# Channel mixing's first layer by fifteen products for 3x3x2 blocks, and forms of both layers' weights in one series

## The chip, the cores and the metric

The kernel runs on one core of a Trainium2 chip, as one launch. The metric is the device time of one execution in microseconds (us), the median of several runs. TensorE (PE) does the matmuls, VectorE (DVE), ScalarE (ACT) and GpSimd (POOL) the elementwise work, and SyncE (SP) issues most transfers.

## The reference

Attention with normalized queries and keys for 8 batch elements and 12 heads (448 positions, 64 wide), then a mixer over its result, all in float32:

```python
q_n, k_n = (rmsnorm(q, g_q), rmsnorm(k, g_k))        # over the 64
scores = scale * np.matmul(q_n, k_n.transpose(0, 1, 3, 2))
attn = softmax(scores); attn_out = np.matmul(attn, v)
x = attn_out.transpose(0, 2, 1, 3).reshape(8, 448, 768)
xt = x.transpose(0, 2, 1)
h = np.maximum(xt @ w_tok1, 0.0) @ w_tok2            # token mixing, 448 -> 256 -> 448
u = x + h.transpose(0, 2, 1)
h2 = np.maximum(u @ w_ch1, 0.0) @ w_ch2              # channel mixing, 768 -> 1536 -> 768
return u + h2
```

The mixer's weights arrive as float64.

## The kernel before

The elements go through one after another. For each: attention in six blocks of two heads (scores L458, exponentials on ACT L462, row sums of them added on DVE in `es` L499, the product with v L531; then the sums' transpose `dt` L560, reciprocal `rc` L562, its transpose `rd` L574 and the scaled result `uT` L577); `x` in the other orientation through DRAM (`send_x` L786, `load_x` L795); token mixing `tok1` (L837, L844) and `tok2` (L879, drained at L884); channel mixing `ch1` (L999) and `ch2` (L1065). The attention of the next element is laid between the products of channel mixing, in blocks: `place` puts the six blocks ahead of the products whose numbers `BLOCKS` lists, counted over both layers. Each of PE, DVE, ACT and POOL works in the order in which the program is written. `later(t, fn)` puts off work to a time of a modelled PE clock, and the order in SP's queue is set by a planner from such times.

Element 0's channel mixing is plain (`first_stage`, L969, 36 products): meanwhile float64 weights are loaded (`weight_load` L222, into five `raw` tiles) and converted on DVE and ACT (L345 to L379). Converted weights go to DRAM scratch (`store`), and come back as units of 384 KB (`unit`, L927, eight buffers).

From element 1 on `ch1` is made in 3 times 7 products of 12 matmuls of 224 columns, the products of a 2x2x2 block scheme. For these, sums of weights are made once on POOL (`sum_items`; the first eight, `few`, in tiles of the pool of `x` during element 0, with loads on POOL's own queue), and sums of the moving data each element (`moving_sums` L900 to L904, tile `tu`). Results pile up by `PRODUCTS` in `hb` and `r`; drains on DVE (L1005), copies on ACT (L1009, L1021), relu on ACT (L1006).

`ch2` is plain in element 1 (`plain_2`, L1048), and from element 2 on 15 products of 8 matmuls of 224 columns, for 3x3x2 blocks: `ch2(b, f, x)` for f in 0 to 14 and x in 0, 1, drained by `C_STEPS[f]` (L1076, L1080). Its moving operands, forms of the hidden layer, are made in place by `x_form` (L1039, 896 elements) as `X_STEPS` lists them; the first four of them are written after products 0, 2, 3 and 5 of the last block of `ch1`. The forms of its weights (8 groups of 16 operations and 4 copies, L320, L324, sent at L310) are made on POOL in `form_items`, during element 1.

Two pools of PSUM tiles matter here: `m_tile` (two tiles; all products of `ch1` and `ch2`) and `s_tile` (four; scores and transposes). `put_off` holds back work until the next product's matmuls are written.

Of the kernel before, what the change touches and what calls it, by code (L numbers as in the profile page):

```python
# [8 lines left out]
F32 = mybir.dt.float32  # L9
# [13 lines left out]
NQ = 8  # L23
NF9 = 15
# [16 lines left out]
    ("ch1", 0): (("v", 6, 1, "+", 3),), ("ch1", 2): (("v", 7, 6, "+", 0),),  # L41
    ("ch1", 3): (("g", 9, 0, "+", 1),), ("ch1", 5): (("v", 8, 7, "+", 2),),
# [20 lines left out]
    (("v", (1, 0), (1, 0), "+", "P"),))  # L63

# [19 lines left out]
def whole(ctx, tc, shifted, pre, q, k, v, g_q, g_k, moe_w_tok1, moe_w_tok2, moe_w_ch1, moe_w_ch2, out):  # L84
# [10 lines left out]
    P = 128  # L95
# [52 lines left out]
    ws1 = dram.tile([KF // 2, NQ, P, KC, 2, P], F32, name="ws1")  # L148
# [76 lines left out]
    def slots(j, lo, hi):  # L225

        w, group, m, t = stages[j]
        return ws1[group, lo:hi, :, t, m % 2, :].rearrange("q p n -> p q n")

    def store(j):  # L230

        w, group, m, t = stages[j]
        if group < 3:
            nc.sync.dma_start(out=slots(j, 0, 4), in_=st["stage", j])
            return
        to = wp2[:].rearrange("p (m q t) n -> p q m t n", m=KC, q=4)[:, :, m, t, :]
        nc.sync.dma_start(out=to, in_=st["stage", j])

    def has(group, made):
        return all(j in made for j, s in enumerate(stages) if s[1] == group)  # L240

    def sum_items():


        n = len(stages)

        def make(e, a, q):

            e.tensor_tensor(out=q[:, 6], in0=a[:, 1], in1=a[:, 0], op=ALU.subtract)
            e.tensor_tensor(out=q[:, 4], in0=a[:, 1], in1=a[:, 3], op=ALU.add)  # L250
            e.tensor_tensor(out=q[:, 5], in0=q[:, 6], in1=a[:, 3], op=ALU.add)
            e.tensor_tensor(out=q[:, 7], in0=a[:, 2], in1=q[:, 5], op=ALU.subtract)

        def send(i, e=nc.sync):
            st["summed"].add(i)
            e.dma_start(out=slots(i, 4, 8), in_=eight(st.pop(("sum", i)))[:, 4:8])


        FEW = 8

        def some(i):
            if 2 <= i:
                send(i - 2, nc.gpsimd)
            if i < FEW:
                t = st["sum", i] = x_pool.tile([P, KC, NS, P], F32, name="few", tag="x")
                nc.gpsimd.dma_start(out=eight(t)[:, 0:4], in_=slots(i, 0, 4))
            if 1 <= i <= FEW:
                q = eight(st["sum", i - 1])
                make(nc.gpsimd, q, q)

        order = list(range(FEW, n // 2))

        def one(i):
            if i < len(order):
                t = st["sum", order[i]] = raw_tile()
                nc.sync.dma_start(out=eight(t)[:, 0:4], in_=slots(order[i], 0, 4))
            if 0 <= i - 2 < len(order):
                q = eight(st["sum", order[i - 2]])
                make(nc.gpsimd, q, q)
            if 0 <= i - 3 < len(order):  # L280
                send(order[i - 3])
                load_units(st["at"])

        def eight(t):
            if len(t.shape) == 4:
                return t[:].rearrange("p j c n -> p (j c n)")[:, 0:NQ * P].rearrange("p (q n) -> p q n", q=NQ)
            return t[:].rearrange("p n w -> p (n w)").bitcast(F32).rearrange("p (q n) -> p q n", q=NQ)
        return ([(0.0, lambda i=i: some(i)) for i in range(FEW + 2)],
                [(1.0, lambda i=i: one(i)) for i in range(len(order) + 3)])

    def form_items():


        G, FORMS_FROM, FORMS_EVERY = range(8), 55.0, 18.0
        plain = lambda g: wp2[:].rearrange("p (m h x k t) n -> p x h t m k n", m=3, h=2, x=2, k=3)[
            :, g // 4, g // 2 % 2, g % 2]
        made = ws2[:].rearrange("p (f c) n -> p c f n", c=8)
        eight = lambda t: t[:].rearrange("p n w -> p (n w)").bitcast(F32).rearrange("p (q n) -> p q n", q=8)

        def load(g):  # L300
            a, b, c = st["form", g] = [eight(raw_tile()) for _ in range(3)]
            src = plain(g)
            for m in range(2):
                nc.sync.dma_start(out=a[:, 3 * m:3 * m + 3], in_=src[:, m])
            nc.sync.dma_start(out=a[:, 6:8], in_=src[:, 2, 0:2])
            nc.sync.dma_start(out=b[:, 7], in_=src[:, 2, 2])

        def send(g):
            a, b, c = st.pop(("form", g))
            nc.gpsimd.dma_start(out=made[:, g, 0:8], in_=c)  # L310
            nc.gpsimd.dma_start(out=made[:, g, 8:NF9], in_=b[:, 0:7])
            st["formed"] += 1

        def part(g, i):
            a, b, c = st["form", g]
            at = dict(d=a[:, 4], s=a[:, 6], v=a[:, 7], y=a[:, 3])
            at.update({(m, k): a[:, 3 * m + k] if 3 * m + k < 8 else b[:, 7] for m in range(3) for k in range(3)})
            at.update({f: c[:, f] if f < 8 else b[:, f - 8] for f in range(NF9)})
            for o, x, op, y in W_STEPS[4 * i:4 * i + 4]:
                nc.gpsimd.tensor_tensor(  # L320
                    out=at[o], in0=at[x], in1=at[y], op=ALU.add if op == "+" else ALU.subtract)
            if i == 3:
                for f, x in W_SINGLE:
                    nc.gpsimd.tensor_copy(out=at[f], in_=at[x])  # L324
                send(g)

        for g in G:
            at = FORMS_FROM + g * FORMS_EVERY
            later(at, lambda g=g: load(g))
            for i in range(4):  # L330
                later(at + 8.0 + 2.5 * i, lambda g=g, i=i: part(g, i))
# [472 lines left out]
    def trans_x(b, j):  # L804
# [20 lines left out]
        if o == KC - 1:  # L825
            t = st["xt"][:, half].rearrange("p j s -> p (j s)")
            if half:
                st.pop("xt")
            start, step, load = {(1, 1): (2.0, 0.5, 9.0), (2, 1): (2.0, 0.5, 9.0)}.get((b, half), (2.0, 2.0, 12.0))
            later(start, lambda: send_x(b, half, t, step))  # L830
            later(load, lambda: load_x(b, half))
# [58 lines left out]
    PRODUCTS = ((0, "B11"), (2, "B21"), (5, "T2"), (6, "T3"), (4, "T1"), (7, "B22"), (3, "T4"))  # L890

    def moving_sums(b, t):

        if t == 0:
            st["tu"] = tu_pool.tile([P, 4, KC, HS], F32, name="tu", tag="tu")
        u, tu = st["uT", b], st["tu"]
        B11, B12 = u[:, t, 0:HS], u[:, t, HS:S]
        B21, B22 = u[:, KC + t, 0:HS], u[:, KC + t, HS:S]
        T1, T2, T3, T4 = (tu[:, i, t, :] for i in range(4))
        nc.vector.tensor_tensor(out=T1, in0=B12, in1=B11, op=ALU.subtract)  # L900
        nc.vector.tensor_tensor(out=T2, in0=B22, in1=T1, op=ALU.subtract)
        e = nc.vector if b == 1 else nc.gpsimd
        e.tensor_tensor(out=T3, in0=B12, in1=B22, op=ALU.subtract)
        e.tensor_tensor(out=T4, in0=B21, in1=T2, op=ALU.subtract)  # L904

    def unit_list(b):

        flat = lambda a: a.rearrange("p a b n -> p (a b n)")
        l = [(mp, q < 4, flat(ws1[mp, q])) for mp in range(KF // 2) for q, _ in PRODUCTS]
        six = lambda w, i: w[:, 6 * i:6 * i + 6, :].rearrange("p a n -> p (a n)")  # L910
        if b == 1:
            return l + [(3, True, six(wp2, mt % KC * 4 + 2 * h + mt // KC)) for mt in order_2 for h in range(2)]
        return l + [(4, False, six(ws2, i)) for i in range(NF9 * 8 // 6)]

    def load_units(u):
# [3 lines left out]
        while ("stage", len(stages) - 1) in st["used"] and st["loaded"] < min(u + UNITS - 1, len(units)):  # L919
            i = st["loaded"]  # L920
            group, plain, src = units[i]

            if not plain and not (has(group, st["summed"]) if group < 3 else st["formed"] == 8):
                assert i > u
                break
# [61 lines left out]
    def ch1(b, mp, i):  # L987

        put_off_done()
        u, tu = st["uT", b], st["tu"]  # L990
        ps = m_tile()
        w = next_unit()
        q, what = PRODUCTS[i]
        for j in range(2):
            for t in range(KC):
                m = {"B11": u[:, t, 0:HS], "B21": u[:, KC + t, 0:HS], "B22": u[:, KC + t, HS:S]}.get(what)
                if m is None:
                    m = tu[:, int(what[1]) - 1, t, :]
                nc.tensor.matmul(  # L999
                    out=ps[:, j * HS:(j + 1) * HS], lhsT=w[:, t, j, :], rhs=m,  # L1000
                    start=(t == 0), stop=(t == KC - 1))
        got = ps[:, 0:2 * HS]
        h = {name: hb[:, 2 * mp + n, 2 * o:2 * o + 2, :].rearrange("p m n -> p (m n)")
             for name, o, n in (("B11", 0, 0), ("B12", 0, 1), ("B21", 1, 0), ("B22", 1, 1))}
        add = lambda e, o, x, y: e.tensor_tensor(out=o, in0=x, in1=y, op=ALU.add)  # L1005
# [520 lines left out]
```

## Time and profile before

| | us |
|---|---|
| median of 3 runs | 1286.82 (1285.78 to 1289.69) |
| profiled execution, its own time | 1290.15 |
| its span, first to last instruction | 1288.2 |
| PE busy | 1251.4 |
| DVE busy | 794.4 |
| ACT busy | 392.2 |
| POOL busy | 381.7 |

The mean granted clock of TensorE was 0.994. Element 0 ends at about 262 us, element 1 at about 424, and each of elements 2 to 6 takes about 148. The profile is of one execution; "busy" is the time in which an engine has an instruction in work, and a group's line gives its count, its busy time and the mean of one in ns, and then the engine's idle time ahead of it with what ended that.

### The profile page before, as it was taken

What the parts mean: (1) busy time and instruction counts of PE and PEld (TensorE: products, weight loads), DVE (VectorE), ACT (ScalarE), POOL (GpSimd) and SP (SyncE); (2) the same over time, 40 slices, a digit from 0 to 9 for tenths busy, and PEclk for the clock granted to TensorE, in tenths of its full rate; (3) what the DMA queues carried; (4) which work ended last, traced back from release to release, by engine and by line L of the source; (5) the groups of instructions that cost most, each with busy time, mean ns of one, the idle gap of its engine ahead of it and who ended that gap; (6) DMA issues with size and microseconds to landing.
All of it is one profiled execution on the core that took longest, in us unless ns stands there. A gap on an engine that the chain in (4) does not pass through costs nothing.

```text
span 1288.2 us, 20010 instructions
## 1 busy us (share of the span) xinstructions
PE 1251.4 (97%) x7228; PEld 890.5 (69%) x7228; DVE 794.4 (62%) x1229; ACT 392.2 (30%) x781; POOL 381.7 (30%) x641
## 2 busy tenths in 40 slices
PE   5998999999999999999999999999999999999996
PEld 3444444457744488796778777885787868797996
DVE  6987877846764355855668356765658366544243
ACT  5663333223331144402442043312343033200210
POOL 1303350024996611331223112241122222131231
PEclk9998999999999999999999999999999999999999
DMA  9666494999899876695658767685766864386553
GB/s 209 170 183 184 124 258 115 208 253 250 225 249 239 182 170 165 141 253 116 160 148 184 183 147 179 146 231 115 178 163 149 223 146 135 117 210 156 173 173 82
DMA packets 492864, 228.37 MB, mean 177 GB/s; under 512 B 375508, under 2 KB 453332, under 8 KB 492756
## 3 DMA queue, kind: packets, MB, share of 16 engines
q1 hardware_dynamic: 476178, 213.10, 67.2%
q0 software_dynamic: 3584, 12.06, 3.1%
q10 hardware_dynamic: 12994, 1.84, 0.8%
q8 instruction: 59, 0.97, 0.3%
q14 instruction: 49, 0.40, 0.1%
HBM read 184.26 MB, written 42.66 MB: 176 GB/s over the span
## 4 chain that ended last, share of the span: by engine, by line
PE 84%; DVE 7%; DMA 3%; SPq 2%; issue 1%; ACT 1%; POOL 0%; DVEq 0%; ACTq 0%; POOLq 0%
PE m_ps L999 25%; PE m_ps L1065 21%; PE s_ps L458 9%; PE o_ps L531 9%; PE m_ps L879 5%; PE m_ps L969 5%; PE t_ps L837 2%; PE m_ps L837 2%; PE m_ps L1048 1%; PE m_ps L511 1%; PE d_ps L511 1%; DMA x<-xs 1%; PE t_ps L432 1%; DVE es L499 1%; DVE raw L348 1%
## 5 line engine op out<-in xcount | busy, mean ns | idle before, releaser
L1065 PE MATMUL m_ps<-hb,unit 128*128 128x224 f32 x1440 | 277.2, 354 | 0.0
L1065 PEld LDWEIGHTS m_ps<-hb,unit 128*128 128x128 f32 x1440 | 270.9, 190 | 8.8 <-issue 7.7
L999 PE MATMUL m_ps<-tu,unit 128*128 128x224 f32 x1008 | 201.6, 355 | 1.3 <-ACT r L1009 1.3
L999 PEld LDWEIGHTS m_ps<-tu,unit 128*128 128x128 f32 x1008 | 189.1, 190 | 15.0 <-issue 9.2
L462 ACT ACTIVATE e<-s_ps 128x448 f32<-128x448 f32 x294 | 138.2, 550 | 179.1 <-PE s_ps L458 170.7
L999 PE MATMUL m_ps<-uT,unit 128*128 128x224 f32 x756 | 151.2, 354 | 0.3 <-DVE hb L1005 0.3
L999 PEld LDWEIGHTS m_ps<-uT,unit 128*128 128x128 f32 x756 | 142.2, 190 | 7.4 <-issue 3.9
L458 PE MATMUL s_ps<-qkT 64*64 64x448 f32 x1260 | 143.9, 545 | 0.8 <-ACT x L819 0.8
L531 PE MATMUL o_ps<-e,v 64*64 64x448 f32 x1148 | 129.7, 538 | 0.3 <-ACT uT L568 0.2
L499 DVE TENSOR_TENSOR es<-es,e 128x896 f32<-128x896 f32 x90 | 102.8, 1142 | 14.6 <-ACT e L462 9.3
L1005 DVE TENSOR_TENSOR hb<-m_ps,r 128x448 f32<-128x448 f32 x63 | 39.1, 621 | 109.3 <-POOL r L1005 56.7
L1005 POOL TENSOR_TENSOR hb<-r,r 128x448 f32<-128x448 f32 x21 | 23.9, 1138 | 243.8 <-ACT r L1021 243.8
L458 PEld LDWEIGHTS s_ps<-qkT 64*64 64x64 f32 x1260 | 45.4, 132 | 69.5 <-issue 60.4
L531 PEld LDWEIGHTS o_ps<-e,v 64*64 64x64 f32 x1148 | 45.6, 133 | 62.3 <-issue 58.7
L879 PE MATMUL m_ps<-w_sb,h 128*128 128x448 f32 x192 | 77.3, 555 | 3.6 <-DVE uT L884 3.6
L1006 ACT ACTIVATE hb<-hb 128x448 f32<-128x448 f32 x84 | 48.4, 577 | 100.4 <-DVE hb L1005 78.3
L1438 POOL TENSOR_TENSOR nt<-rs 128x56 f32<-128x56 f32 (+1 forms) x57 | 19.4, 341 | 197.2 <-DVE rs L1430 194.2
L320 POOL TENSOR_TENSOR raw<-raw 128x128 f32<-128x128 f32 x128 | 66.7, 541 | 31.4 <-DMA raw<-wp 26.9
L1080 POOL TENSOR_TENSOR uT<-uT,r 128x448 f32<-128x448 f32 x42 | 51.4, 1238 | 78.5 <-DVE r L1080 46.7
L1005 DVE TENSOR_TENSOR r<-m_ps,r 128x448 f32<-128x448 f32 x42 | 26.1, 622 | 64.1 <-PE m_ps L999 64.1
L884 DVE TENSOR_TENSOR uT<-uT,m_ps 128x448 f32<-128x448 f32 x48 | 29.3, 613 | 59.0 <-PE m_ps L879 59.0
L1408 DVE TENSOR_REDUCE ms<-sq 128x28 f32<-128x896 f32 (+2 forms) x44 | 47.4, 1080 | 27.7 <-ACT sq L1394 24.3
(141 smaller groups left out, 1591.0 us busy)
## 6 DMA issues: line engine op xcount, KB each, us to landing
unit<-ws SPq DMA_DIRECT2D x267, 384.0 KB, 3.9
raw<-in_moe_w_ch_dram SPq DMA_DIRECT2D x72, 256.0 KB, 3.4
v<-in_v_dram SPq DMA_DIRECT2D x96, 112.0 KB, 3.7
xs<-xt SPq DMA_DIRECT2D x56, 168.0 KB, 4.6
out_dram<-turned SPq DMA_DIRECT2D x168, 56.0 KB, 2.0
qk_t<-in_q_dram SPq DMA_DIRECT2D x144, 56.0 KB, 3.4
qk_t<-in_k_dram SPq DMA_DIRECT2D x144, 56.0 KB, 3.6
x<-xs SPq DMA_DIRECT2D x42, 192.0 KB, 3.9
```

What stands on the lines that cost most here:

```text
L320: nc.gpsimd.tensor_tensor(out=at[o], in0=at[x], in1=at[y], op=ALU.add if op == "+" else ALU.subtract)
L458: nc.tensor.matmul(out=pss[i][rows_of(i, a), 0:S], lhsT=qkT[h, 1, k * D:(k + 1) * D], rhs=qkT[h, 0, :], start=True, stop=True)
L462: nc.scalar.activation(out=e[:, i, :], in_=pss[i][:, 0:S], func=AF.Exp)
L499: nc.vector.tensor_tensor(out=es[:], in0=(es if k > 1 else st["e", t, 0])[:], in1=st["e", t, k][:], op=ALU.add)
L531: nc.tensor.matmul(out=st["o", p][a * D:(a + 1) * D, 0:S], lhsT=vt[rows, k * D:(k + 1) * D], rhs=e[rows, :], **kw)
L837: nc.tensor.matmul(out=st["t1", h][jc][:, 0:HC], lhsT=w1_sb[:, c, jc * P:(jc + 1) * P], rhs=st["x", b, h][:, :, c, :], start=start and c = ...
L879: nc.tensor.matmul(out=ps[:, 0:S], lhsT=st["h1", jc][:, cc * P:(cc + 1) * P], rhs=w2_sb[:, jc].rearrange("p c r -> p (c r)"), start=(jc == ...
L969: nc.tensor.matmul(out=ps, lhsT=a[:, o + 2 * half, :], rhs=natural(half * KF + t) if wide else u[:, half * KC + t, :], start=(t == 0 and h ...
L999: nc.tensor.matmul(out=ps[:, j * HS:(j + 1) * HS], lhsT=w[:, t, j, :], rhs=m, start=(t == 0), stop=(t == KC - 1))
L1005: add = lambda e, o, x, y: e.tensor_tensor(out=o, in0=x, in1=y, op=ALU.add)
L1065: nc.tensor.matmul(out=ps[:, x * HS:(x + 1) * HS], lhsT=st["w"][:, tile_at % 6, :], rhs=hb[:, X_SLOT[f], i, :], start=(i == 0), stop=(i == 3))
L1080: e.tensor_tensor(out=get(out), in0=get(x_), in1=get(y), op=ALU.add if op == "+" else ALU.subtract)
```

## The change

From element 2 on, `ch1(b, f, o)` makes the first layer by 15 products too, f in 0 to 14 and output half o in 0, 1; the product for o = 0 goes into a tile of the pool of scores (`c_ps`), that for o = 1 into one of `m_tile`'s two. `C1_STEPS` lists the drains, `RELU` where a block of the hidden layer is done, `X1_STEPS` the forms of the moving data, made by `pre_forms` during `tok2` and by `x1_forms` between products. Element 1's first layer is plain (`plain_1`: 12 units of 6 matmuls of 448 columns). `X_STEPS` now begins the second layer's forms after products (12, 1), (13, 0), (13, 1) and (14, 0).

The sums of weights are gone. `form(layer, g, small)` makes a group of 15 forms for either layer; there are 16 groups. The first four are made during element 0, in two tiles of the pool of `x` each, loaded on SP's queue; the other twelve in `raw` tiles during element 1. `BLOCKS` changes for the new count of products, and `send_x`/`load_x` of element 2's second half have earlier times. The plain weights of the first layer get a DRAM tensor of their own, `wp1`.

```diff
 X_STEPS = {
-    ("ch1", 0): (("v", 6, 1, "+", 3),), ("ch1", 2): (("v", 7, 6, "+", 0),),
-    ("ch1", 3): (("g", 9, 0, "+", 1),), ("ch1", 5): (("v", 8, 7, "+", 2),),
+    ("ch1", 12, 1): (("v", 6, 1, "+", 3),), ("ch1", 13, 0): (("v", 7, 6, "+", 0),),
+    ("ch1", 13, 1): (("v", 8, 7, "+", 2),), ("ch1", 14, 0): (("g", 9, 0, "+", 1),),
...
+X1_STEPS = {
+    ("pre", 0): (("v", 0, (0, 1), "+", (1, 1)), ("v", 1, 0, "+", (0, 0))),
+    ("pre", 1): (("g", 3, (0, 0), "+", (0, 1)), ("v", 2, 1, "+", (1, 0))),
+    (0, 0): (("v", 4, 3, "-", (2, 1)),), (1, 0): (("v", 5, 4, "-", (2, 0)),), (1, 1): (("v", 0, 5, "+", (1, 0)),),
+    (2, 1): (("g", 1, (0, 1), "-", (2, 1)),), (5, 0): (("v", 2, 0, "-", 1),), (7, 0): (("g", 4, 0, "+", (1, 1)),)}
+
+C1_STEPS = (
+    (("a", (2, 1), "P", None, None),),
+    (("v", "A", (2, 1), "-", "P"),),
...
+    (("v", "A", "A", "-", "P"), ("v", (2, 1), (2, 1), "+", "A")),
+    (("v", "A", "A", "+", "P"), ("v", (1, 0), "B", "+", "A"), ("v", (1, 1), (1, 1), "-", "A")),
+    (("v", (1, 0), (1, 0), "+", "P"),))
+RELU = {5: (0, 0), 8: (0, 1), 11: (2, 0), 12: (2, 1), 13: (1, 1), 14: (1, 0)}
...
-    def sum_items():
...
-        G, FORMS_FROM, FORMS_EVERY = range(8), 55.0, 18.0
...
+    def form(layer, g, small):
...
+            else:
+                a, c = [x_pool.tile([P, KC, NS, P], F32, name="form", tag="x")[:].rearrange("p a c n -> p (a c) n")
+                        for _ in range(2)]
...
+            nc.sync.dma_start(out=flat[:, 0:6 * P].rearrange("p (m n) -> p m n", m=2), in_=rows(0, 2))
...
+    FIRST_FORMS = 4
+    def later_forms():
+        for i in range(16 - FIRST_FORMS):
+            n = FIRST_FORMS + i
+            at = 14.0 * i if i < 3 else 28.0 + 20.0 * (i - 2)
+            load, *parts = form(1 + n // 8, n % 8, True)
+            later(at, load)
+            for k, fn in enumerate(parts):
+                later(at + 8.0 + 2.5 * k, fn)
...
-            start, step, load = {(1, 1): (2.0, 0.5, 9.0), (2, 1): (2.0, 0.5, 9.0)}.get((b, half), (2.0, 2.0, 12.0))
+            start, step, load = {(1, 1): (2.0, 0.5, 9.0), (2, 1): (0.0, 0.25, 6.0)}.get((b, half), (2.0, 2.0, 12.0))
...
-    def moving_sums(b, t):
...
-    def ch1(b, mp, i):
+    def ch1(b, f, o):
         put_off_done()
+        ps = m_tile() if o else s_tile("c_ps")
...
+        for eng, out, a, op, c in C1_STEPS[f]:
+            if op is None:
+                nc.scalar.copy(out=at[out], in_=at[a])
+                continue
+            e = nc.gpsimd if eng == "g" else nc.vector
+            e.tensor_tensor(out=at[out], in0=at[a], in1=at[c], op=ALU.add if op == "+" else ALU.subtract)
...
+        put_off(lambda: x1_forms(b, (f, o)))
+        for step in X_STEPS.get(("ch1", f, o), ()):
+            put_off(lambda step=step: x_form(*step))
+
+    def plain_1(b, m, half):
...
-            if j % 2 and j < 2 * len(some):
-                items.append(some[j // 2])
+            if 0 <= j - 10 < 4 * FIRST_FORMS:
+                g, i = divmod(j - 10, 4)
+                items += [(0.0, fn) for fn in [forms[g][0:1], [], forms[g][1:3], forms[g][3:]][i]]
...
-    BLOCKS = (0, 6, 11, 17, 23, 31)
+    BLOCKS = (0, 9, 16, 25, 33, 41)
```

In the changed kernel's own lines, the first layer's matmul is L987, its copies L997, its drains L1000 and its relu L1004; the second layer's matmul is L1055, its drains L1070; element 0's products are L955.

## The prediction

> **What bounds the kernel now.** I read the page first, its busy line, its chain and its groups.
>
> ```profile
> PE 1251.4 (97%) x7228; PEld 890.5 (69%) x7228; DVE 794.4 (62%) x1229; ACT 392.2 (30%) x781; POOL 381.7 (30%) x641
> ...
> PE 84%; DVE 7%; DMA 3%; SPq 2%; issue 1%; ACT 1%; POOL 0%; DVEq 0%; ACTq 0%; POOLq 0%
> ...
> L1065 PE MATMUL m_ps<-hb,unit 128*128 128x224 f32 x1440 | 277.2, 354 | 0.0
> ...
> L999 PE MATMUL m_ps<-tu,unit 128*128 128x224 f32 x1008 | 201.6, 355 | 1.3 <-ACT r L1009 1.3
> ...
> L999 PE MATMUL m_ps<-uT,unit 128*128 128x224 f32 x756 | 151.2, 354 | 0.3 <-DVE hb L1005 0.3
> ```
>
> PE is the bound: 97% busy, and channel mixing's two layers (L999, L1065) are half of it. Each fp32 matmul is two records; a 224-column record costs 277.2 / 1440 = 0.1925 us at L1065 and 352.8 / 1764 = 0.2000 at L999 (that count has the start-up of each stretch in it; inside one, consecutive records start 0.1905 apart). Fewer records are therefore time won, if PE still finds its operands. Next, what PE waits for.
>
> ```profile
> PE t_ps L432 <- DVE g_t L1193: 15.0, 1, 15.0
> PE m_ps L879 <- DVE uT L884: 3.6, 3, 2.8
> PE t_ps L844 <- DMA x<-xs: 2.2, 1, 2.2
> PE m_ps L999 <- ACT r L1009: 1.3, 1, 1.3
> ...
> PE m_ps L969 <- DVE stage L379: 0.7, 1, 0.7
> ```
>
> After the start (15.0) PE waits for next to nothing; L1065 waits for no drain at all. The slack under that is in the busy times by stretch: an element's first layer with its four attention blocks, its second layer with two, the last element's first layer with none, and the end of element 0.
>
> ```profile
> 743.20:814.70 71.50, 71.50 (x493) 56.25 (x493) 44.29 (x62) 30.08 (x61) 14.27 (x21) 1.00 0.66 164
> 814.70:872.40 57.70, 57.70 (x362) 49.49 (x361) 41.37 (x63) 13.20 (x27) 19.47 (x33) 1.00 0.78 196
> 1184.20:1232.00 47.80, 47.80 (x254) 47.79 (x253) 13.29 (x20) 9.54 (x17) 10.11 (x9) 1.00 0.61 184
> ...
> 203.00:252.00 49.00, 48.53 (x175) 22.71 (x173) 46.78 (x85) 15.15 (x25) 5.07 (x4) 1.00 0.80 192
> ```
>
> DVE (third busy figure) has room in an element, 44 of 71.5 us, but none from 203 to 252: 46.78 of 49, the weights' conversion, with PE just behind it (the 0.7 us wait on L379).
>
> **The change, part by part.**
>
> *PE's records.* Elements 2 to 7: 15 products of 8 matmuls are 120, 240 records, for 126 and 252: 12 × 0.1905 = 2.29 us less each, 13.7 in all. Element 1 goes from 252 such records (48.3 us at 0.1915, between the two rows' spacings) to 72 matmuls of 448 columns, 144 records; by L1048, 55.2 us for the same 144, 54.4 by spacing: +6.1. Together −7.6 us. Drains and forms add DVE work (32 drains and 7 forms an element where 15 and some 12 small ones were), about +55 us in all, 794 to about 849; by stretch 44 of 71.5 becomes about 55 of 69, so no bound by itself.
>
> *x of element 2.* Its second half is sent from 0.0 instead of 2.0 and loaded at 6.0 instead of 9.0. The wait at L844 is 2.2 us, the most to be won; I take −1.5.
>
> *The handover from the first layer to the second.* Here I see the largest cost. The four forms of the hidden layer that the second layer's products need first (slots 6, 7, 8 on DVE, 9 on POOL) are now made after products (12,1), (13,0), (13,1), (14,0); before, after four of the last block's seven products. In the changed order of instructions, the fourth attention block lies ahead of (12,1), so its DVE work lies between the last drains. DVE runs in written order. Durations:
>
> ```profile
> L499 DVE TENSOR_TENSOR es<-es,e 128x896 f32<-128x896 f32 x90 | 102.8, 1142 | 14.6 <-ACT e L462 9.3
> ...
> L1039 DVE TENSOR_TENSOR hb<-hb 128x896 f32<-128x896 f32 x42 | 46.0, 1094 | 0.4 <-POOL hb L1039 0.3
> ...
> L574 DVE STREAM_TRANSPOSE rd<-rc 128x448 f32<-128x448 f32 x48 | 30.1, 627 | 0.0
> ...
> L577 DVE TENSOR_TENSOR uT<-o_ps,rd 128x448 f32<-128x448 f32 x42 | 26.2, 625 | 1.5
> ```
>
> with a drain of 448 elements at 0.62 (0.55 when the next follows at once, 0.65 when it needs the one before), dt with rc 0.84, rd with uT 1.25. Let E be PE's end of (12,1); DVE starts 0.3 later. In order: two drains to E+1.5; two es to 3.7; form 6 to 4.7; three drains of (13,0) to 5.9; dt and rc to 7.1; form 7 to 8.3; then the first drain of (13,1) at 8.3 to 8.9. That drain frees the second layer's first buffer (pool M has two). PE has only four units of 8 × 0.1905 = 1.52 until then and is there at E+6.1: it waits 2.85 us. DVE goes on: two more drains of (13,1), dt, rc, form 8 to 10.9; (14,0) to 11.9; two small ones, rd, uT, then (14,1)'s drain to 14.6. PE wants that buffer for its second product (two units of 1.52) at 8.95 + 3.05 = 12.0: it waits 2.7. So 5.55 us in each of elements 2 to 5; 4.0 in element 6 (fewer blocks' operations, one es less ahead of form 6); 1.25 in element 7 (no block, only drains and forms): 22.2 + 4.0 + 1.25 = +27. Bounds: if half the block's operations are done earlier than I place them, 14; if it is all as written, 27. I take 27, since each item is a row.
>
> *The clock.* Two PE waits of 2.8 us within 6 us are a thing that the trace has one by one:
>
> ```profile
> 338.00:342.00 4.00, 2.70 (x15) 2.36 (x14) 3.29 (x4) 3.17 (x8) 3.90 (x5) 1.00 0.98 259
> ...
> 429.10:431.40 2.30, 0.10 (x3) 0.06 (x1) 0.00 (x0) 0.87 (x2) 2.06 (x6) 1.00 1.15 277
> ...
> 433.00:436.40 3.40, 3.40 (x6) 1.70 (x6) 0.65 (x1) 0.29 (x1) 1.22 (x2) 0.51 0.89 199
> ```
>
> A wait of 1.3 us (first row) left the clock (the third column from the end) at 1.00; the 2.2 us one is followed 1.6 us later by 3.4 us at 0.51, and a 2.77 us gap at 110 us by 6.8 us at half. So a stall of 2.8 us may cost 1.7 us (half of 3.4) or 3.4 more. What falls on the first product is hidden by the second stall; what follows the second is not. Bounds for five elements: 0, and 5 × 3.4 = 17. I take +6, near 5 × 1.7 less the one or two that a gap misses.
>
> By the Trainium skill (TensorE: Matmul & The Clock Gate, "Why this matters for your kernels") a PE-idle gap has to exceed some 3 us before the clock drops, so gaps of 2.8 us would cost nothing and the sum would be 6 us lower. The rows above speak against that here, since 2.2 us was enough.
>
> *Element 0.* The first four forms of the weights read their plain weights over SP's queue (POOL's queue before) into two tiles of a pool of two. So the load of forms 1, 2 and 3 waits on SP for the sends of the one before, about 9 us of POOL later, and x of element 1 waits for the last; behind them in SP's order stand the loads of raw weights.
>
> ```profile
> L320 POOL TENSOR_TENSOR raw<-raw 128x128 f32<-128x128 f32 x128 | 66.7, 541 | 31.4 <-DMA raw<-wp 26.9
> ...
> raw<-in_moe_w_ch_dram SPq DMA_DIRECT2D x72, 256.0 KB, 3.4
> ```
>
> One form is 16 such operations and four copies, 9.8 us with its two sends' issue after. From the positions, SP stands from about 148 to 163 and 167 to 182, and x of (1,0), loaded at 224.8 before, goes out about 236; the weights behind it land near 244 where DVE wanted them from 233 on (its one wait for raw weights now: 0.6 us at 233.1). DVE has 2.2 of 49 us to catch up in. I take +9; bounds 0, if five raw tiles cover it, and 14, if both earlier waits add.
>
> *Element 1's forms.* Twelve forms of about 11.2 us are 134 us of POOL in a window of about 156 (from 288 to 424 us POOL is busy for 99 of 136 now): covered; if it weren't, the reciprocal roots on POOL (L1438) would be 2 to 3 us late, which attention's scale has in hand. Price 0, up to 5.
>
> Sum: −7.6 − 1.5 + 27.4 + 6 + 9 = +33.3. The profiled execution took 1290.15 us (span 1288.2 and 1.95 around it), 3.3 above the median of 1286.82; so 1323.5 for such a run, and 1320 beside the median.
>
> **The rivals.**
>
> *Faster: the handover does not bind.* If the block's es and transposes are done before E, and element 0's queue has room, only the records count: −7.6 − 1.5 = −9, 1278. For it: L1065 never waited for a drain. Against: the order is written, and DVE's items between E and the second product's buffer sum to 14.4 us against 9.1 of PE. It decides below 3 us of stall in all, for then neither clock nor weights can outweigh it. Chance 0.1.
>
> *The handover alone:* no clock loss, element 0 covered: −9 + 27 = +18, 1305. For it: gaps below 3 us, five raw tiles. Chance 0.3.
>
> *All as priced:* 1320, chance 0.4. *Everything at its upper bound:* −9 + 27 + 17 + 14 + 5 = +54, 1341; chance 0.15, for two stalls close together may keep the clock down for two windows.
>
> *The stall at half size* and nothing else: −9 + 14 = +5, 1292; chance 0.05, of which most is no change.
>
> **How the numbers follow.** A measurement of this kernel can tell about 0.3%, 3.9 us. Likeliest 1320; range 1294 to 1342, from the half-sized stall to all bounds, which leaves out the faster rival and a little above. Faster 0.11, same 0.05, slower 0.84.
>
> **What would show it.** In the profile after: PE busy 1244 plus what runs at half clock; DVE near 849; a wait of the second layer's matmul (L1055) for drains at L1000 of about 5.5 us an element in four of them; a granted clock below 0.994; PE's wait for the converted weights (L955) between 235 and 275, of some 9 us. If PE waits at L1055 are below 1 us an element, the handover step is wrong and the time lies at 1278 to 1290; if element 0 ends at 262 as before, its term is.

## The result, and the profile after

The changed kernel takes 1381.41 us (median of 4 runs, 1375.85 to 1382.60) against 1286.30 for the kernel before on the same chip: the ratio is 1.0727, 95% interval 1.069 to 1.0765. It is slower, as forecast, but by 95 us and not by 33, and the time lies outside the range. The profiled execution has a span of 1380.5 us, 92.3 more than before.

From the page of the changed kernel, the busy times and the chain that ended last:

```profile
PE 1277.1 (93%) x7048; PEld 877.8 (64%) x7048; DVE 867.3 (63%) x1310; ACT 401.6 (29%) x775; POOL 435.1 (32%) x697
...
PE 59%; DVE 15%; POOL 11%; DMA 7%; issue 3%; SPq 3%; ACT 1%; DVEq 0%; POOLq 0%; ACTq 0%
```

PE has 180 records fewer and is busy for 26 us more, part of it at half clock; its share of the chain fell from 84% to 59%, and POOL, which had 0% of it, has 11%. PE's waits over the whole run, without the 15.0 us of the start (total, times, longest):

```profile
PE m_ps L943 <- ACT r L954: 14.3, 2, 13.8
PE m_ps L1055 <- DVE r L1000: 13.2, 6, 2.8
PE m_ps L1055 <- DVE hb L1000: 13.1, 6, 3.4
PE o_ps L522 <- DMA v<-in_v_dram: 11.7, 1, 11.7
PE m_ps L1055 <- DVE r L1070: 6.9, 4, 1.7
PE m_ps L1038 <- DVE uT L1043: 5.8, 2, 3.5
PE m_ps L943 <- ACT hb L957: 4.8, 1, 4.8
```

L943 is element 0's matmul (L955, named for it ahead of the prediction and in its signs, is POOL's addition of the result), L522 attention's product with v, laid into element 0; L1038 is element 1, L1055 the second layer from element 2 on. To see where the 92 us lie I took the start of each element's token mixing from the trace and the differences:

| element | before, us | after, us | difference |
|---|---|---|---|
| 0 | 261.8 | 298.4 | +36.6 |
| 1 | 162.5 | 176.3 | +13.8 |
| 2 | 152.4 | 161.0 | +8.6 |
| 3, 4, 5 | 147.8, 147.9, 147.9 | 156.2, 158.7, 155.8 | +8.4, +10.8, +7.9 |
| 6 | 145.4 | 151.4 | +6.0 |
| 7 | 122.5 | 122.7 | +0.2 |

Half of the loss is in elements 0 and 1, where the first layer's fifteen products don't run. What SP waits for between 140 and 280 us, from the changed kernel's list of waits of the DMA queue:

```profile
SPq L294 <- DMA ws<-form: 20.9, 1, 20.9
SPq L295 <- DMA ws<-form: 15.8, 1, 15.8
SPq L786 <- DMA ws<-form: 15.7, 1, 15.7
```

These are the three places that the prediction named: the loads of forms 1 and 2 and that of x behind form 3, each behind the send (`ws<-form`) of the form before. What stood behind them in SP's order reached PE by three ways. PE's wait at 187 us is for v of the next element, issued on SP at 194.7. That at 212 is for ACT's drain of a product (L957), which stands in ACT's order behind the squares of the next keys; these landed at 214.9. That at 263 is for ACT's copy of a result (L954), which stands behind its part of the conversion, and there DVE waited for raw weights (from 255 to 277 us):

```profile
DVE cv_sb L336 <- DMA raw<-in_moe_w_ch_dram: 15.5, 1, 15.5
```

In element 3 the handover looks like this, by windows (PE busy is the second figure, DVE busy the fourth; the granted clock stands third from the end): wait, first product, wait.

```profile
725.98:728.77 2.79, 0.01 (x2) 0.01 (x1) 2.72 (x6) 0.00 (x0) 0.00 (x0) 1.00 0.63 178
728.77:733.74 4.97, 4.97 (x16) 4.27 (x16) 4.90 (x9) 0.95 (x1) 2.34 (x1) 0.66 0.09 9
733.74:735.48 1.74, 0.01 (x2) 0.01 (x1) 1.71 (x4) 0.02 (x1) 1.39 (x5) 1.00 0.56 201
```

DVE is busy in both waits nearly without a gap. Between them 16 records take 4.97 us instead of 3.05: the half clock. Elements 2 and 5 are alike; in element 4 the clock stayed at 1.00 between the waits, and the second is 3.42 us.

### The profile page after: what moved, and what is told of

Read it like the earlier page. It is cut to its first block, busy times and chain, and to the rows that moved or that the text cites. A ratio compares the mean times of both kernels' runs of the same rounds, so it can differ in the third digit from the quotient of the medians.

```text
span 1380.5 us, 19642 instructions
## 1 busy us (share of the span) xinstructions
PE 1277.1 (93%) x7048; PEld 877.8 (64%) x7048; DVE 867.3 (63%) x1310; ACT 401.6 (29%) x775; POOL 435.1 (32%) x697
## 4 chain that ended last, share of the span: by engine, by line
PE 59%; DVE 15%; POOL 11%; DMA 7%; issue 3%; SPq 3%; ACT 1%; DVEq 0%; POOLq 0%; ACTq 0%
PE m_ps L1055 17%; PE c_ps L987 8%; PE m_ps L987 8%; PE s_ps L449 7%; POOL raw L300 6%; PE o_ps L522 6%; PE m_ps L870 4%; POOL form L300 3%; PE m_ps L943 3%; DVE es L490 2%; PE t_ps L828 2%; DVE hb L1000 2%; DVE hb L1029 2%; PE m_ps L828 2%; DMA raw<-in_moe_w_ch_dram 1%
## 5 line engine op out<-in xcount | busy, mean ns | idle before, releaser
L1055 PE MATMUL m_ps<-hb,unit 128*128 128x224 f32 x1440 | 287.1, 361 | 33.1 <-DVE r L1000 13.2
L1055 PEld LDWEIGHTS m_ps<-hb,unit 128*128 128x128 f32 x1440 | 276.2, 194 | 47.1 <-DVE r L1000 15.2
L449 PE MATMUL s_ps<-qkT 64*64 64x448 f32 x1260 | 160.1, 552 | 0.8 <-ACT x L810 0.8
L522 PE MATMUL o_ps<-e,v 64*64 64x448 f32 x1148 | 142.4, 541 | 12.0 <-DMA v<-in_v_dram 11.7
L490 DVE TENSOR_TENSOR es<-es,e 128x896 f32<-128x896 f32 x90 | 109.0, 1211 | 15.7 <-ACT e L453 10.4
L300 POOL TENSOR_TENSOR raw<-raw 128x128 f32<-128x128 f32 x192 | 102.1, 553 | 44.2 <-DMA out_dram<-turned 37.6
L987 PE MATMUL m_ps<-tu,unit 128*128 128x224 f32 x480 | 102.1, 355 | 0.0
L987 PE MATMUL c_ps<-tu,unit 128*128 128x224 f32 x480 | 101.2, 354 | 0.0
L522 PEld LDWEIGHTS o_ps<-e,v 64*64 64x64 f32 x1148 | 52.2, 133 | 73.1 <-issue 48.7
L987 PEld LDWEIGHTS m_ps<-tu,unit 128*128 128x128 f32 x480 | 89.7, 190 | 8.2 <-issue 6.3
L987 PEld LDWEIGHTS c_ps<-tu,unit 128*128 128x128 f32 x480 | 90.4, 190 | 4.3 <-ACT e L453 3.1
L1029 POOL TENSOR_TENSOR hb<-hb 128x896 f32<-128x896 f32 x18 | 39.7, 2208 | 151.5 <-DVE hb L1000 102.1
L969 POOL TENSOR_TENSOR tu<-uT 128x448 f32<-128x448 f32 x12 | 13.6, 1135 | 217.4 <-DVE uT L875 123.8
L943 PE MATMUL m_ps<-hb,stage 128*128 128x448 f32 x144 | 61.1, 584 | 19.4 <-ACT r L954 14.3
L1070 POOL TENSOR_TENSOR uT<-uT,r 128x448 f32<-128x448 f32 x42 | 54.7, 1317 | 73.0 <-DVE r L1070 42.9
L411 DVE TENSOR_TENSOR qk_t<-qk_t,rs 128x896 f32<-128x896 f32 (+1 forms) x42 | 56.1, 1374 | 26.0 <-POOL rs L1432 26.0
```

The costliest lines, as they stand in the source:

```text
L300: nc.gpsimd.tensor_tensor(out=at[o], in0=at[x], in1=at[y], op=ALU.add if op == "+" else ALU.subtract)
L411: nc.vector.tensor_tensor(out=x, in0=x, in1=r.unsqueeze(2).to_broadcast(list(x.shape)), op=ALU.mult)
L449: nc.tensor.matmul(out=pss[i][rows_of(i, a), 0:S], lhsT=qkT[h, 1, k * D:(k + 1) * D], rhs=qkT[h, 0, :], start=True, stop=True)
L490: nc.vector.tensor_tensor(out=es[:], in0=(es if k > 1 else st["e", t, 0])[:], in1=st["e", t, k][:], op=ALU.add)
L522: nc.tensor.matmul(out=st["o", p][a * D:(a + 1) * D, 0:S], lhsT=vt[rows, k * D:(k + 1) * D], rhs=e[rows, :], **kw)
L943: nc.tensor.matmul(out=ps, lhsT=a[:, o + 2 * half, :], rhs=natural(half * KF + t) if wide else u[:, half * KC + t, :], start=(t == 0 and h ...
```

## The experiments

All are the changed kernel with the edit named; times are medians of 4 runs with the kernel before beside them on the same chip (its medians: 1286.9 to 1288.0).

**Element 0: the tiles of the forms.** `e1_unit` moves the first four forms from the pool of x into the eight unit buffers.

```diff
-                a, c = [x_pool.tile([P, KC, NS, P], F32, name="form", tag="x")...
+                t = [unit_pool.tile([P, 3, 2, P], F32, name="unit", tag="unit")... for _ in range(4)]
```

> The first four forms are made in four tiles each of the weights' units (eight buffers, unused in element 0), so that a form's load waits for the send of the form before the last one, and x of element 1 for none. Theory (SP's queue stands behind the sends: 20.9, 15.8 and 15.7 us in the trace of the changed kernel): element 0 ends at 262 to 268 us instead of 298, the time falls by 28 to 36 us, to 1345 to 1353. Rival (POOL's or DVE's added work in element 0 is late by itself, and SP's standing is only its mark): element 0 ends after 290, the time falls by less than 8.

It took 1380.49 us (ratio 1.071, 1.0681 to 1.074), as if nothing had been done; element 0 ended at 296.1. But the expectation's "unused in element 0" was wrong: the converted weights (`stage`) live in the same buffers. DVE's waits from 140 to 280 us show the new knot:

```profile
DVE stage L375 <- POOL unit L309: 21.9, 2, 20.1
DVE stage L375 <- POOL unit L305: 10.1, 1, 10.1
```

DVE's conversion waits for POOL to be done with a form, where before SP did. So this run, whose time is the rival's by number, does not speak for the rival's cause; it exchanged one wait for another of like size.

**Element 0: the queue.** `e1b_poolq` leaves the tiles and issues these loads on POOL's queue.

```diff
-            nc.sync.dma_start(out=flat[:, 0:6 * P]..., in_=rows(0, 2))     # and two more
+            e = nc.sync if small else nc.gpsimd
+            e.dma_start(out=flat[:, 0:6 * P]..., in_=rows(0, 2))           # and two more
```

> Only the queue of the first four forms' loads is changed, from SP's to POOL's; they stay in the two tiles of the pool of x. Theory (SP stands behind the sends twice, and once for x of element 1, which needs a tile that form 3 holds until about 256 us): PE's waits at 187 and 212 us (11.7 and 4.8) go, the one at 263 (13.8) stays, since x still waits for form 3's tile; element 0 ends at 278 to 284 instead of 298, 1362 to 1368. Rival (POOL's forms in front of its other work in element 0, the additions of the second layer's results at L955, make the waits, whoever loads): waits of together 25 us or more stay, 1375 or more.

1362.3 us (ratio 1.0578, 1.0552 to 1.0603), and element 0 ended at 280.0: PE's waits at 187 and 212 us are gone, one of 3.4 came at 219, and that at 246 (263 before) is there with 12.1 us. SP now waits once for a form's send, at x:

```profile
SPq L787 <- DMA ws<-form: 12.8, 1, 12.8
```

**Element 0: the queue, and one form fewer.** `e5_pool3` has POOL's queue, three first forms and the later ones 24 us apart.

```diff
-    FIRST_FORMS = 4
+    FIRST_FORMS = 3
-            at = 14.0 * i if i < 3 else 28.0 + 20.0 * (i - 2)
+            at = 24.0 * i
```

> The first forms' loads on POOL's queue, three of them in element 0 instead of four, and the thirteen later ones 24 us of the modelled clock apart. Theory (queue order and the tile that x waits for): element 0 ends at 261 to 268 us, element 1 takes 165 to 168; 1335 to 1345. Rival (POOL's load in element 0): element 0 still ends after 285.

1345.06 us (ratio 1.0444, 1.0419 to 1.0469): element 0 ends at 265.6 and element 1 takes 166.3, as expected. So 33 of element 0's 36.6 us are gone: 18 with the queue alone (e1b), and 14 more with one form fewer, which both frees the tile that x waited for and takes some 10 us of POOL's work out of element 0; these two were not tested apart. Element 2 rose to 167.5 us; some of the later forms are now made in it. The remaining wait (3.4 us at 219) is for ACT's copy of a result. In the trace that copy stands in ACT's order behind the scaling of a qkT, which waits for DVE's transposes until 220.9, while POOL was done with its form by 213.7. With two first forms (`g4`, `h1` to `h3` below) the wait is gone, and element 0 ends at 258.6 to 259.1, before the 261.8 of the kernel before.

**Element 1.** `e3_spread` changes only the modelled times of the twelve later forms.

```diff
-            at = 14.0 * i if i < 3 else 28.0 + 20.0 * (i - 2)
+            at = 26.0 * i
```

> Only the modelled times of the twelve later forms are changed, to 26 us apart (14, then 20). Theory (with forms 11.5 us apart SP stands 3 to 11 us for raw tiles at each form's load, and units and q/k come late behind it): the two waits of PE in element 1's second layer (5.8 us) and the half clock after them (3.4) go, and element 1 takes 165 to 168 us instead of 176; 1370 to 1373. Rival (these waits are for DVE's addition of uT, as the list of waits names it): no change, within 3 us of 1381.

1376.14 us (ratio 1.0677, 1.0649 to 1.0706). Element 1 fell from 176.3 to 166.3, as the theory said, with no wait left at L1038; the whole fell by only 5 us, for element 2 rose from 161.0 to 162.4, with two waits of 2 us in its first layer while forms are made there, and element 0 came out 1.8 longer. SP's waits for raw tiles, from 300 to 480 us, in the changed kernel and then in this one:

```profile
SPq L294 <- DMA ws<-raw: 61.2, 9, 10.8
```

```profile
SPq L294 <- DMA ws<-raw: 18.7, 2, 10.4
```

The list of waits named DVE's addition of uT for PE's wait at L1038, and rightly: in the changed kernel PE went on at 451.2 us, when that addition ended. But DVE was busy for only 1.6 of those 3.5 us. Ahead of the addition in its order stood a sum of squares, which waited for ACT, and ACT for the next keys; their loads had gone out behind a form's on SP. The waits from 445 to 467 us:

```profile
ACT sq L1385 <- DMA qk_t<-in_k_dram: 29.0, 2, 18.1
...
DVE ms L1399 <- ACT sq L1385: 24.0, 2, 13.8
```

**The handover: blocks.** `e2_blocks` moves the attention blocks only.

```diff
-    BLOCKS = (0, 9, 16, 25, 33, 41)
+    BLOCKS = (0, 7, 14, 20, 33, 40)
```

> Only BLOCKS is changed, to (0, 7, 14, 20, 33, 40): the fourth attention block five products earlier, the sixth one product earlier. Theory (DVE's items of the fourth block between the last drains make the handover's wait, and the sixth block's place the later wait of 1.7 us): elements 2 to 6 keep a handover wait as element 7 has it (2.6 us) and lose the third wait; 5 us less in each of elements 2 to 5 and 3 in element 6, 23 in all, 1358. Rival (the drains and the three forms alone fill DVE after (12,1)): under 6 us in all, 1376 or more.

1371.61 us (ratio 1.0666, 1.0625 to 1.0708), between the two: 10 us less, where the theory had 23. The later wait of 1.7 us (L1070) is gone, elements 3 to 5 take 153.9, but the handover kept waits of 2.69 and 1.38 with half clock between: es had left the chain, and drains, forms, `rd` and `uT` fill it all the same.

**The handover: the order of the forms.** `e6_xsteps` has these blocks, makes the forms later, and form 9 on DVE instead of POOL:

```diff
-    ("ch1", 12, 1): (("v", 6, 1, "+", 3),), ("ch1", 13, 0): (("v", 7, 6, "+", 0),),
-    ("ch1", 13, 1): (("v", 8, 7, "+", 2),), ("ch1", 14, 0): (("g", 9, 0, "+", 1),),
+    ("ch1", 13, 0): (("v", 6, 1, "+", 3),), ("ch1", 13, 1): (("v", 7, 6, "+", 0),),
+    ("ch1", 14, 1): (("v", 8, 7, "+", 2), ("v", 9, 0, "+", 1)),
```

> BLOCKS (0, 7, 14, 20, 33, 40) and besides the second layer's first forms in another order: 6 after the drains of (13,0), 7 after those of (13,1), 8 and 9 after (14,1), 9 on DVE too. Theory (DVE's chain from (12,1) to (14,1) makes the wait: two drains, the wait for a relu, form 6, and form 8 at 2.98 us instead of 1.08 because POOL makes form 9 at the same time): the handover's 6 us (2.7 + 1.4 of waits, 1.9 of half clock) fall to 0 to 2 in elements 2 to 6 and 0 in element 7; against the kernel with these BLOCKS alone (1371.6) 25 to 34 less, 1338 to 1347. Rival (the number of drains itself fills DVE): 5 to 10 less, 1362 to 1367.

1348.9 us (ratio 1.0478, 1.0454 to 1.0502), 22.7 less than with the blocks alone: a little short of the theory's 25 to 34 and far more than the rival's 5 to 10. How much of it is the order and how much form 9's engine, this run can't tell. Elements 3 to 5 take 150.5, the handover waits 1.06 and 1.31, and the clock stays up. PE's waits there in all elements:

```profile
PE m_ps L1055 <- DVE hb L1000: 6.4, 5, 1.3
PE m_ps L1055 <- DVE r L1000: 4.8, 5, 1.1
```

**The tiles of the scores.** `e4_m` puts all products of the first layer into pool M.

```diff
-        ps = m_tile() if o else s_tile("c_ps")
+        ps = m_tile()
```

> The first layer's products all go into the two tiles of pool M; the scores keep their four. Theory (c_ps takes a score tile, so that the score matmuls of two heads no longer start together: 9.63 us for 80 records in an element's first layer, 8.00 before): the score matmuls come back to 0.100 us each, 1.6 us an element less, and PE does not wait for drains outside the handover; 1373 (8 less). Rival (with two tiles PE waits for DVE's drains whenever a block's row sums are queued ahead of them): 1.5 to 4 us an element more, 1385 to 1405.

1405.73 us (ratio 1.0922, 1.0893 to 1.0952). The theory's 1373 did not come; the time is at the upper end of the rival's range. Both mechanisms showed: the 80 score records of an element's first layer went back to 0.100 us each, and PE waits for drains with only two tiles, 7 us an element, with half clock after some of the waits:

```profile
PE m_ps L987 <- DVE r L1000: 18.4, 12, 2.1
PE m_ps L987 <- DVE hb L1000: 17.2, 15, 1.5
```

So the pool of scores is needed, and costs 1.6 us an element.

**Together.** `e7_all` is `e5_pool3` and `e6_xsteps` with the third block at 12.

> Both together, and the third block at 12 instead of 14. If the parts add up: 1371.6 less 30 (handover) less 40 (elements 0 and 1), about 1300. The block at 12: products (5,0) and (5,1) ahead of it have one drain by ACT each, so that the score tiles are free and the matmuls of two heads start together; 0.8 us an element less. Rival (what is late next, DVE in the element as a whole, takes back half): 1315 or more.

1312.41 us (ratio 1.0188, 1.0163 to 1.0212), between sum and rival. Clock and element 0 are mended; elements 3 to 5 take 151.2 to 151.8. The block at 12 was worse than that at 14, not 0.8 us better: PE spends 1.2 us more on the attention of the first layer's blocks than before the change (0.9 in e6), and waits 1.65 us for ACT behind the fourth (0.65 in e6).

**Places of the blocks.** Four more with the forms in the new order: `g1` BLOCKS (0, 7, 18, 30, 35, 40), `g2` (0, 7, 14, 22, 30, 38), `g3` (0, 7, 18, 24, 30, 40), `g4` as g2 with two first forms.

> The joint kernel (loads on POOL's queue, three first forms, later ones 24 apart, the forms 6 to 9 reordered) with BLOCKS (0, 7, 18, 30, 35, 40): the fourth block lies between the two layers. Theory (a block's 5.4 us of matmuls there let DVE work off the last drains): no wait at the handover (2.4 us in the joint kernel), and the block at 18, behind products with one drain each, without the loss of 0.9; but three blocks follow in 13 products, and DVE has some 16 us for each 13. An element 148 to 151 us, 1298 to 1312. Rival (DVE is late in the second layer instead): 152 us or more, over 1313.

> As g1 with BLOCKS (0, 7, 14, 22, 30, 38): evenly 7 to 8 products apart, the fifth block between the layers. Theory (as in g1, and DVE's work is spread): no handover wait, 147 to 149 us an element instead of 151.7, 1290 to 1298. Rival (score tiles held by c_ps at blocks 14 and 22 cost 1 us each, as in the joint kernel): 149 to 151, 1300 to 1310.

> As g1 with BLOCKS (0, 7, 18, 24, 30, 40): the third block behind (8,1), the fourth behind (11,1). Theory: blocks at 18 and 24 follow products with one or two drains by DVE; if what the products just ahead leave in DVE's and ACT's queues decides on the score tiles, the block at 18 costs 5.4 to 6.2 and that at 24 6.5 to 7 us of PE; 148 to 150 an element, 1293 to 1303. Rival (any block amid the first layer but the first two loses 1 us): as g2 or more.

> As g2, but two first forms in element 0 instead of three and the fourteen later ones 22 apart. Theory (the one wait left in element 0, 3.4 us at 219, is for ACT's copy that waits for POOL's addition behind the third form, and half clock after it costs 2): element 0 ends at 261 to 262 instead of 265.6. Against it: one more form in elements 1 and 2. The same as g2 within 4 us. Rival (POOL is full in elements 1 and 2): 5 to 10 more than g2.

g1 took 1311.28 (ratio 1.0182), g2 1334.83 (1.0366), g3 1332.64 (1.0352), g4 1331.77 (1.0352). g1 is at the border of its theory and its rival: its elements 3 to 5 take 151.1 to 153.0, and the handover's wait is gone, but waits of 1.5 us for score tiles and of some 2.5 us for the second layer's drains came instead. g2 and g3 are misses for theory and rival alike: a block at 30 that follows another within eight products waits 5 us for score tiles amid its matmuls (longest wait 4.95, at s_ps), and half clock follows. The block at 18 was clean in g1 and g3 (6.18 us of PE, as before the change), that at 22 or 24 was not (PE waits 0.7 to 1.2 us for ACT behind it). g4 against g2 is level in elements 1 to 6 and gains in element 0 only.

Then three runs on what is left in elements 2 to 6: `h1` (0, 7, 18, 32, 37, 42), `h2` (0, 7, 14, 20, 33, 40), `h3` (0, 7, 18, 22, 33, 40), all with two first forms 22 apart.

> Two first forms, later ones 22 apart, forms 6 to 9 reordered, BLOCKS (0, 7, 18, 32, 37, 42): three blocks in each layer, none within 11 products ahead of the handover, and blocks only where the products ahead left the score tiles free in earlier runs (7 and 18). Theory (what is left per element, 2.6 to 3.8 us over the kernel before, is wait for DVE behind a block at the handover and score tiles held by c_ps): the first layer's part without waits, 240 records as in element 7; but three blocks in the second layer's 13 products; 146 to 149 us an element, 1282 to 1296. Rival (DVE's total in the element is what binds, wherever the blocks lie): 150 or more, 1300 and over, with the waits now at the second layer's drains.

> As h1 with BLOCKS (0, 7, 14, 20, 33, 40), those with which an element took 150.5 us. Theory (parts add up): 258.6 and 166.3 for elements 0 and 1 as with two first forms before, some 160 for element 2, 150.5, 147 and 121 for the rest: 1304, within 4 us. Rival (one more form in elements 1 and 2 fills POOL): 1310 or more.

> As h1 with BLOCKS (0, 7, 18, 22, 33, 40): the third block behind (8,1) and the fourth only four products later. Theory (a block costs more where c_ps is held by a late drain, and four products are too few for DVE to work off a block): the third costs 6.2, the fourth over 7, and the handover waits 2 to 4 us; 151 to 154 an element, 1305 to 1320. Rival (places behind single drains suffice): 148 to 150, 1292 to 1302.

h1 took 1315.4 us (ratio 1.0224, 1.0196 to 1.0251), 153.7 to 154.1 in elements 3 to 5. Its first layer and its handover are nearly clean (0.78 us of wait), and the wait stands in the second layer instead, as the rival had it: 4.9 us in each of four elements, behind three blocks:

```profile
PE m_ps L1056 <- DVE r L1071: 19.7, 4, 4.9
```

The window of one such wait:

```profile
713.60:718.50 4.90, 0.00 (x0) 0.00 (x0) 4.69 (x13) 0.00 (x0) 2.24 (x8) 1.00 0.77 134
```

PE does nothing in it, and DVE is busy for 4.69 of 4.90. h3 took 1327.64 (1.0317), more than theory and rival had; its elements 3 to 5, 153.3 to 154.8, are the theory's, but element 2 took 169.4. h2, the parts already measured, came out as the sum said: 1306.79 us (ratio 1.0157, 1.0129 to 1.0185), with no PE work at half clock:

```profile
PE 1249.9 (96%) x7048; PEld 859.1 (66%) x7048; DVE 857.4 (66%) x1316; ACT 401.6 (31%) x775; POOL 426.8 (33%) x697
```

It is the best version with the change, 75 us under the changed kernel, and 19 over the one before. By the profiles, whose spans are 13 apart, it is over by 3.8 in element 1, 5.9 in element 2, 2.6 in each of elements 3 to 5 and 1.6 in element 6, and under by 3.2 in element 0 and 2.5 in element 7.

## Why the prediction was wrong, step by step

| term | forecast, us | measured |
|---|---|---|
| records, elements 2 to 7 | −13.7 | −2.3 in element 7's first layer (47.5 to 45.2 us): right |
| records, element 1 | +6.1 | +5.1 with the waits away (h2: 166.3 for 162.5, which held a wait of 1.3) |
| x of element 2 | −1.5 | 0: the wait is 2.14 for 2.20 |
| handover waits | +27 | +26.3: 13.2 and 13.1 |
| a third wait (L1070) | none | +6.9 |
| score tiles held by c_ps | none | +1.6 in each of five elements, 8 |
| clock | +6 | +18 |
| element 0's waits | +9 | +29.7: 11.7, 4.8 and 13.8, less 0.7 before |
| element 1's waits | 0, up to 5 | +4.5: 3.5 and 2.3, less 1.3 before |

With the first row as forecast, the measured column sums to 85 of 92 us; the other 7 lie in PE's busy time and have no cause here. The clock's row is half of PE's busy time in the stretches at half clock, 22.7 us against 4.8.

**Element 0 is the step that failed.** Mechanism and places were right: SP stands behind the sends of forms, e1b shows it, and its waits of 20.9, 15.8 and 15.7 us are those foreseen with 15, 15 and 11. What was mis-sized is what they cost: +9, with 14 as the upper bound, against 29.7 us of PE's waits. The sum priced the third wait alone, through weights that land late near 244, and gave the first two nothing unless both added up. But behind those two stood v and the keys of the next element, which no term had: PE waited 11.7 us at 187 and 4.8 at 212. The raw weights behind x cost 13.8 at 263. So PE waited 30 us for SP's 52. The bound should have been the sum of SP's waits, 41 us by the prediction's own figures, since the page showed DVE without slack there.

**The handover's waits** came to 26.3 us for 27.4, but the sum is closer than its parts: 4.4 to 4.5 in elements 2, 3 and 5 and 6.0 in element 4 where 5.55 was forecast, 4.4 in element 6 (4.0) and 2.7 in element 7 (1.25). That they cancel is luck. The mechanism held: in element 3 the first product's wait is 2.8 (2.85), and E to the second product 15.6 us (14.7). The difference is form 8, which took 2.14 us there and in element 7 2.98, where the sum had 1.08. Three times in between (5.9, 7.1 and 10.9) are less than the durations beside them add up to; the trace has 6.6, 7.4 and 13.0, the last with 1.06 for the longer form 8. The two times on which the waits rest, 8.9 and 14.6, agree with it but for that 1.06: 8.9 and 15.6.

The Trainium skill (SBUF — State Buffer, "SBUF: two separate sides") says that a DVE operation with two inputs in SBUF and a POOL operation that reads SBUF take turns at a shared pair of ports, whole instructions at a time. The trace agrees: in element 7 POOL's form 9 ran from 1323.3 us for 2.34, form 8 started at 1323.6 on DVE, and it ended 0.95 us after form 9 did, nearly its own length. The second wait is smaller than forecast where the first product ran at half clock before it, which the prediction foresaw; in element 4, where it ran at full clock, the second wait is 3.42.

**DVE's work** was sized too small: 867.3 us for the forecast 849, and 106.7 in each of elements 2 to 5 for 92.5. The count of some 12 small operations an element before was too high, for the moving sums on DVE (L900, L901) are 42 in seven elements, 6 in each, so that less fell away.

**The clock** is the other mis-sized term, +18 us for +6. Each of the five handovers in elements 2 to 6 was followed by half clock, for 3.4 us in four and 6.8 in one, and this cost 9.8 us of the 18; 5 came from the waits in element 0 and 3 from element 1, which had not been costed with waits at all. The prediction's reading of the rows against the page's rule held: waits below 3 us are enough. In the changed kernel half clock followed four of the five handover waits of 2.6 to 2.8 us (in element 4 it came only after the second wait, of 3.42), and at the handovers of e6 and h2, with waits of 1.06 and 1.31, there was none.

**Element 1** failed by the same omission as element 0: POOL's time was counted (134 us, measured 132 from first to last load), the queue that its tiles block was not. SP waited 61 us for raw tiles, the next keys stood behind it, and DVE's addition behind the keys.

**The rivals.** None of them held the time; "everything at its upper bound", 1341, came nearest. The third wait and the score tiles are 15 us that no rival had. The faster one was wrong by its own test, DVE's items between E and the second product.

What is not settled is whether some order of blocks brings elements 2 to 6 below the 147.9 us of the kernel before. Seven were tried with the new order of forms; the best takes 150.5. In e6 these 150.5 hold 3.3 us in which PE is idle; h1 shows that emptying the first layer of blocks moves the wait into the second. DVE's work in an element is 105 to 107 us against 92.5, and that it binds everywhere is argued from this, not shown. For it speaks that the change pays where DVE has less to do: element 7, without blocks, takes 120.0 in h2 for 122.5, and element 6, with one block fewer, 143.3 in h1 (though 146.9 in h2) for 145.3.

## What to carry to other kernels

Before a load is put on a shared queue, list what it waits for and everything behind it on that queue, chain by chain, and bound the cost by the whole wait for each chain without slack. Fewer matmuls are worth their records only if their drains fit where they land: here 12 records an element (2.3 us) bought 17 drains of 0.6 us on an in-order engine. And a tile borrowed from a pool, for scores or for forms, lends its waits to that pool's other users.

## What was not expected of the hardware

In all seventeen traces, from 60 us on, 65 of the 83 TensorE waits of 2.6 to 5.5 us saw the granted clock fall to half during them or within 4.5 us of their end, mostly for 3.4 or 6.8 us; so did 23 of the 40 from 2.0 to 2.6 us, and 2 of the 131 from 1 to 2 us. A stretch of 3.4 us at half, with PE busy in it, costs 1.7. A DVE operation of 896 elements with both inputs in SBUF took up to 2.98 us instead of 1.08 when POOL had begun one just before. And the score matmuls of two heads, which start within 0.01 us of each other, fall apart as soon as one of four PSUM tiles is held: 9.63 us for 80 records instead of 8.00, without any wait in the list, since PE counts as busy.
